# Shift taps of all channels as banded 128x128 products on TensorE, the filter loaded first, and a new instruction order

## The chip, the cores and the metric

The kernel runs on one core of a Trainium2 chip. TensorE (PE) multiplies, VectorE (DVE) and ScalarE (ACT) move results out of PSUM and do the elementwise work, GpSimd (POOL) does slower elementwise work, and SyncE (SP) issues the DMA transfers. The metric is the device time of one execution in microseconds. Times inside an execution are counted from the start of the profiled span.

## The reference, cut to what matters

Two kinds of layer alternate, A, B, A, B, over 2048 tokens of 512 channels. A is a gated long convolution: `k` is shifted by a 4-tap causal filter per channel, multiplied by `v`, convolved over the whole sequence with a filter as long as the sequence (plus a diagonal term), and gated by the normalized input. B is an MLP with 1376 hidden units.

```python
def _A_ref(q, k, v, shift_k, ssm_k, ssm_D):
    ...
    for t in range(ks):
        k_shift = k_shift + k_pad[:, t:t + S, :] * shift_k[:, ks - 1 - t][None, None, :]
    kv = k_shift * v
    ...                                    # y = kv convolved with ssm_k by FFT
    y = y + kv * ssm_D[None, None, :]
    return q * y

x = A_q
x = x + _A_ref(_layernorm(x, axis=-1), A_k, A_v, A_shift_k, A_ssm_k, A_ssm_D)
x = x + _B_ref(_layernorm(x, axis=-1), B_w1, B_b1, B_w2, B_b2)
...                                        # the same two once more
```

`k`, `v` and the filters do not depend on `x`, so both A layers share one convolution result Y, which is computed once, at the front.

## The kernel before, in words

**Layout.** A token is 16p + nt: partition p of 128 and row nt of 16. Channels run along the free dimension; they are handled in four tiles of 128, called cc 0 to 3 below, which before are 128 neighbouring channels each. All large buffers are views at fixed byte offsets into one tile, `arena`: `kn` (k), `uv` (v, then k shifted times v), `kT` (k transposed), `Kd` and `Zk` (the long filter), `ZX`, `ZK`, `KSW` (spectra), the MLP weights, and more.

**The front** (up to the first instruction of line L781) is a list of pieces, each with its engine, and with PSUM and SBUF slots; `_Plan.add` names a piece and its dependences, and `_Plan.write` emits the pieces in the order of the string `ORDER`. A word such as `KS60.P0` is piece KS60 on PE with PSUM slot 0; `.D`, `.A`, `.G` and `.S` mean DVE, ACT, POOL and SP. Each engine works strictly in its order of that list; a name with a trailing `e` is the eviction of the piece without it. There are four PSUM slots of 1024 float32 (`p`), nine small buffers `xb` and three large ones `ZT`. The pieces:

- `lk`, `lv`, `lF`, `lK..`, `lW`, `lM`, `lx`, `ly`, `w1` to `w4`: loads of k, v, the Fourier table, the long filter (four loads), the twiddle tables Wt and Mt, the input, the MLP weights. `lSK`, `lh..`: the taps, and k of the rows before.
- `wm0` to `wm2`: matmuls on the identity, without use of the result.
- The filter: `kd` adds the diagonal term to the first tap (32 elements per partition, 128 bytes apart), `KSab` is the first transform stage of 32 channels, 16 matmuls of half width each, `K2j` the second stage, `sa`, `sb` copies of the spectrum with the halves swapped (SBUF to SBUF).
- The taps, cc 0 to 2: `kT` transposes k on PE, `dg` makes diagonal 128x128 matrices of one tap each, `kv` adds up four products per block of tokens in PSUM, `kvm` multiplies the result by v (line L517). `bS` and `bSK` bring the taps into the right partitions. For cc 3: `kg`, `ka` and `kgm` do the multiplications and additions on POOL (L441, L443, L448, L452).
- The data transform of tile cc: `UccS` (four pieces with evictions into `ZT`, L302), `UccT` (turned by PE, or for cc 3 by DMA transposes), then four times `Xccj` (second stage, eviction into `xb`), `Tccj` (product with the filter's spectrum, L559), `Vccj` (inverse stage, L567), `Zccg` or `TD` (turned back), and `Y` (last inverse stage, L633).
- Around Y: `s00`, `s01`, `s02` normalize the first four rows of the input; `g` gates and adds, `h`, `p`, `b` normalize the result (statistics on DVE, power on POOL, application on DVE), `LT` transposes it and `M` is the first half of the first MLP group with its gelu. `LG1`, `q1`, `a1`, `g1.` to `b1.` do the same for the second group.

**The rest** (from L781 on) is written out in a loop over eight groups of 512 tokens, `mm1` (L747 with the gelu L749) and `mm2` (L781, its result added by DVE), four groups for each of the two MLP layers; the first `mm1` is what the pieces M did. The work between two groups (`prep`) belongs to DVE, POOL and SP.

Of the kernel before, what the change touches and what calls it, by code (L numbers as in the profile page):

```python
# [103 lines left out]
def kernel(ctx: ExitStack, tc: tile.TileContext, A_q, A_k, A_v, A_shift_k, A_ssm_k, A_ssm_D,  # L104
# [117 lines left out]
    class Stat:  # L222
# [27 lines left out]
        def apply(self, dst, g, a, b, src=None):  # L250
            for i in range(a, b):
                xs = x_t[:, GT * g + i, :] if src is None else src[:, i, :]
                nc.vector.tensor_scalar(out=dst[:, i, :], in0=xs, scalar1=self.mv[:, i, 0:1], scalar2=self.rs[:, i:i + 1],  # L253
                                        op0=ALU.subtract, op1=ALU.mult)
# [18 lines left out]
    with tc.tile_pool(name="ps", bufs=1, space=bass.MemoryType.PSUM) as ps:  # L273
# [73 lines left out]
        lS = [load("lSK", SKr, apf(A_shift_k, 0, [[D * KS, 1], [1, D * KS]]), 2 ** 13),  # L347
              load("lb1", b1r[:, 0:F], apf(B_b1, 0, [[F, 1], [1, F]]), 2 ** 13)]
        lS += [load(f"lh{p0}", kh[p0:p0 + n, :, :], apf(k_d, (16 * p0 - h) * D + CK * P, [[16 * D, n], [D, h], [1, P]]), 2 ** 17)
               for p0, n in ((1, 112), (113, 15))]  # L350

        def columns(o):
            for ct in range(CK):
                for t in range(KS):
                    nc.tensor.matmul(o[:, ct * KS + t:ct * KS + t + 1], at(81 * K + 2 * (ct * P * KS + t), [[KS, P]], 0, 1),
                                     one[0:1, 0:1], start=True, stop=True)
        _, sf = mm_evac("bS", 700, lS[:1], columns, [CK * KS], lambda: sF[:])

# [55 lines left out]
        for ct in range(CK):  # L414
            def diag(it, ct=ct):
                for t in range(KS):
                    dst, sc = DG[:, ct, t, :], sF[:, ct * KS + t:ct * KS + t + 1]
                    if it["eng"] == "A":
                        nc.scalar.activation(dst, IDt[:], AF.Copy, scale=sc)  # L419
                    else:  # L420
                        nc.vector.tensor_scalar(out=dst, in0=IDt[:], scalar1=sc, scalar2=None, op0=ALU.mult)
            dg.append(plan.add(f"dg{ct}", {"D": 600, "A": 1000}, [sf], diag))
        for q in range(4):
            def mms(o, q=q):
                for i in range(4):
                    for ct in range(CK):
                        nc.tensor.transpose(o[:, i, ct, :], kn[:, 4 * q + i, ct * P:ct * P + P], IDt[:])  # L427
# [5 lines left out]
        c3 = slice(CK * P, D)
        ksum, kpart = kn[:, :, 0:P], kn[:, :, P:2 * P]

        def sk(t, n):
            return apf(SK, t, [[P * KS, P], [0, n], [KS, P]])

        def tap(t):
            m = kpart if t else ksum  # L440
            nc.gpsimd.tensor_tensor(m[:, t:NT, :], kn[:, 0:NT - t, c3], sk(t, NT - t), ALU.mult)  # L441
            if t:
                nc.gpsimd.tensor_tensor(m[:, 0:t, :], kh[:, h - t:h, :], sk(t, t), ALU.mult)  # L443
        kg = []
        for t in range(KS):
            kg.append(plan.add(f"kg{t}", {"G": 4650 if t else 4100}, kg[-1:] if t else lk + lS[2:] + [bSK] + kTp, lambda it, t=t: tap(t)))
            if t:
                kg.append(plan.add(f"ka{t}", {"G": 4100}, kg[-1:], lambda it: nc.gpsimd.tensor_tensor(ksum, ksum, kpart, ALU.add)))  # L448

        def gmul(it):  # L450
            eng = nc.vector if it["eng"] == "D" else nc.gpsimd
            eng.tensor_tensor(uv[:, :, c3], uv[:, :, c3], ksum, ALU.mult)  # L452
# [406 lines left out]
```

## Time and profile before

| | |
|---|---|
| median of 3 runs | 246.73 us (246.53 to 247.12) |
| profiled execution | 246.67 us |
| its span | 244.8 us |
| granted TensorE clock | 1.0 |
| PE, DVE, ACT, POOL busy | 97%, 71%, 55%, 24% of the span |
| first instruction of L781 | 98.83 us |

Rows of the profile are read like this: line, engine, operation, output <- input, shapes, count, then busy time, mean duration of one in ns, and the idle time ahead with what ended it. Rows of the timeline begin with start and duration in us; in the chain, with the start and the time that the piece took in it. Rows of the windows give the stretch, its length, the busy time of PE, weight loads, DVE, ACT and POOL (with the number of instructions), the granted clock, the DMA engines' mean share and GB/s. A duration overlaps the next instruction's start, so the pace of a queue is read from starts.

### The profile page before, as it was taken

How to read it: one execution, taken by the hardware profiler on the slowest of the kernel's cores; microseconds unless marked ns; L12 is line 12 of the kernel's file. 1: busy time of each engine (PE TensorE's matmuls, PEld its weight loads, DVE VectorE, ACT ScalarE, POOL GpSimd, SP SyncE). 2: the span in 40 equal slices, each digit the busy share in tenths (PEclk: the TensorE clock that was granted, in tenths of full speed). 3: DMA queues.
4: the chain of work that ended last, by engine and by line, in shares of the span. 5: the costliest groups of instructions: out<-in, count | busy, mean ns of one | idle time of the engine just before them, and what ended most of it. 6: DMA issues, size and time to landing. Idle time of an engine off the chain costs nothing.

```text
span 244.8 us, 4913 instructions
## 1 busy us (share of the span) xinstructions
PE 236.3 (97%) x2002; PEld 142.0 (58%) x2002; DVE 172.6 (71%) x332; ACT 135.4 (55%) x194; POOL 59.4 (24%) x51
## 2 busy tenths in 40 slices
PE   6999999999997899999999999999999999999994
PEld 2799883789996587444444444444444444444443
DVE  0559699899997989979879898967856951021022
ACT  2538699899998999318307307406505604704700
POOL 2299999760000211310111111011001010000000
PEclk9999999999999999999999999999999999999999
DMA  7999994799998998050400404022024015011011
GB/s 232 329 217 221 170 426 168 265 364 216 260 182 159 269 153 251 3 86 1 85 0 3 87 0 86 3 47 40 0 68 107 0 44 127 3 43 43 0 43 43
DMA packets 56431, 29.64 MB, mean 121 GB/s; under 512 B 48883, under 2 KB 52696, under 8 KB 55514
## 3 DMA queue, kind: packets, MB, share of 16 engines
q1 hardware_dynamic: 56402, 29.34, 48.6%
q8 instruction: 15, 0.25, 0.4%
q14 instruction: 6, 0.05, 0.1%
q10 hardware_dynamic: 8, 0.00, 0.0%
HBM read 15.18 MB, written 2.10 MB: 71 GB/s over the span
## 4 chain that ended last, share of the span: by engine, by line
PE 79%; DVE 9%; ACT 8%; issue 2%; POOL 1%; DVEq 0%; ACTq 0%; POOLq 0%
PE po L781 31%; PE ph L747 27%; DVE arena L212 5%; PE p L509 4%; PE p L691 4%; ACT xb L210 3%; ACT arena L210 3%; PE p L408 2%; ACT ZT L210 2%; PE p L633 1%; PE p L427 1%; PE p L390 1%; PE p L302 1%; PE p L330 1%; DVE ZT L212 1%
## 5 line engine op out<-in xcount | busy, mean ns | idle before, releaser
L749 ACT ACTIVATE arena<-ph,B 128x512 bf16<-128x512 f32 (+1 forms) x77 | 52.8, 687 | 79.5 <-PE ph L747 79.4
L781 PE MATMUL po<-arena 128*128 128x512 bf16 (+2 forms) x363 | 77.4, 373 | 0.0
L747 PE MATMUL ph<-arena 128*128 128x512 bf16 (+1 forms) x308 | 67.6, 379 | 0.0
L781 PEld LDWEIGHTS <-arena 128*128 128x128 bf16 (+1 forms) x363 | 35.4, 98 | 40.6 <-POOL arena L818 0.3
L747 PEld LDWEIGHTS <-arena 128*128 128x128 bf16 (+1 forms) x308 | 30.8, 100 | 35.9
L786 DVE TENSOR_TENSOR arena<-po,arena 128x512 bf16<-128x512 f32 (+1 forms) x33 | 21.5, 671 | 42.6 <-PE po L781 42.5
L210 ACT ACTIVATE arena<-p 128x1024 bf16<-128x1024 f32 (+6 forms) x41 | 37.5, 993 | 8.2 <-PE p L427 5.4
L248 POOL TENSOR_TENSOR lrsm<-lrsm,mhalf 128x4 f32<-128x4 f32 (+2 forms) x11 | 10.1, 920 | 81.3 <-DVE lrsm L242 81.3
L210 ACT ACTIVATE ZT<-p 128x1024 bf16<-128x1024 f32 x21 | 21.5, 1133 | 6.4 <-PE p L302 6.2
L232 DVE BATCH_NORM_STATS2 lstm<-arena 128x6 f32<-128x512 bf16 x32 | 20.0, 681 | 0.3
L232 DVE BATCH_NORM_STATS2 lstg<-arena 128x6 f32<-128x512 bf16 x32 | 19.7, 676 | 0.0
L212 DVE CAST arena<-p 128x1024 bf16<-128x1024 f32 (+1 forms) x17 | 18.0, 1110 | 1.7 <-PE p L374 1.0
L248 POOL TENSOR_TENSOR lrsg<-lrsg,mhalf 128x4 f32<-128x4 f32 x8 | 8.1, 1011 | 43.1 <-DVE lrsg L245 43.0
L559 DVE TENSOR_TENSOR arena<-xb,arena 128x2048 bf16<-128x2048 bf16 (+1 forms) x16 | 17.6, 1151 | 0.9 <-ACT xb L210 0.9
L567 PE MATMUL p<-arena 128*128 128x128 bf16 x256 | 15.8, 219 | 0.5 <-ACT ZT L210 0.3
L441 POOL TENSOR_TENSOR arena<-arena,SK 128x2048 bf16<-128x2048 bf16 (+3 forms) x4 | 15.0, 3753 | 4.2 <-ACT DG L419 4.1
L253 DVE TENSOR_SCALAR arena<-arena,lmvg,lrsg 128x512 bf16<-128x512 bf16 x32 | 11.0, 408 | 6.8 <-POOL lrsg L248 6.8
L210 ACT ACTIVATE xb<-p 128x1024 bf16<-128x1024 f32 x15 | 15.2, 1119 | 0.7 <-PE p L544 0.7
L567 PEld LDWEIGHTS <-arena 128*128 128x128 bf16 x256 | 14.8, 98 | 1.1 <-DVE arena L559 0.5
L253 DVE TENSOR_SCALAR arena<-arena,lmvm,lrsm 128x512 bf16<-128x512 bf16 x32 | 11.5, 416 | 2.2 <-POOL lrsm L248 2.2
L448 POOL TENSOR_TENSOR arena<-arena 128x2048 bf16<-128x2048 bf16 x3 | 12.2, 4068 | 0.2
L509 PE MATMUL p<-DG,arena 128*128 128x128 bf16 x192 | 11.4, 219 | 0.0
(76 smaller groups left out, 224.8 us busy)
## 6 DMA issues: line engine op xcount, KB each, us to landing
arena<-arena SPq DMA_DIRECT2D x8, 512.0 KB, 5.9
arena<-in_A_k_dram SPq DMA_DIRECT2D x2, 1024.0 KB, 6.3
arena<-in_A_v_dram SPq DMA_DIRECT2D x2, 1024.0 KB, 9.6
arena<-in_A_ssm_k_dram SPq DMA_DIRECT2D x4, 512.0 KB, 9.1
arena<-tabM SPq DMA_DIRECT2D x1, 2048.0 KB, 10.3
out_dram<-arena SPq DMA_DIRECT2D x15, 128.0 KB, 1.7
arena<-in_A_q_dram SPq DMA_DIRECT2D x1, 1536.0 KB, 6.8
arena<-in_B_w_dram SPq DMA_DIRECT2D x1, 1376.0 KB, 7.8
```

Source lines behind the costliest of these rows:

```text
L210: nc.scalar.activation(dst, src, AF.Copy)
L212: nc.vector.tensor_copy(dst, src)
L232: nc.vector.bn_stats(self.st[:, i, 0, :], x_t[:, GT * g + i, :] if src is None else src[:, i, :])
L248: nc.gpsimd.tensor_tensor(self.rs[:, a:b], self.rs[:, a:b], mhalf[:, a:b], ALU.pow)
L253: nc.vector.tensor_scalar(out=dst[:, i, :], in0=xs, scalar1=self.mv[:, i, 0:1], scalar2=self.rs[:, i:i + 1], op0=ALU.subtract, op1=ALU.mult)
L509: nc.tensor.matmul(o[:, i, j, :], w, DG[:, cc, t, :], start=t == 0, stop=t == KS - 1)
L559: eng.tensor_tensor(kk, x2, kk, ALU.mult)
L567: nc.tensor.matmul(o[:, i, :], spec[:, cc, ka + i, :], Mt[:, ka + i, r, :], start=r == 0, stop=r == 1)
L747: nc.tensor.matmul(o.rearrange("p (i t) -> p i t", t=P), W1t[:, ct, ft * P:ft * P + m], lt[:, a:b, ct, :], start=ct == 0, stop=ct == CT - 1)
L749: nc.scalar.activation(hT[0:m, ft, a * P:b * P], o, AF.Gelu_apprx_tanh, bias=B1[0:m, ft:ft + 1])
L781: nc.tensor.matmul(po[:, a:b], hT[0:m, ft, i * P:(i + 1) * P], W2t[0:m, ft, a:b], start=ft == 0, stop=ft == FT - 1)
L786: nc.vector.tensor_tensor(xs, po[:, a:b], xs, ALU.add)
```

## The change

- **Tiles of channels.** Tile cc now holds every fourth channel, cc, cc + 4 and so on. Where U reads `uv` it takes `slice(cc, D, 4)`; the filter's KS evictions write `Zk` in that order; and Y, its evictions and the gates bring the channels back (`rows`, `rowd`).
- **Taps.** `kT` now transposes blocks of 4 rows by 32 channels, every 16th channel: 16 blocks for each of four groups of rows q. The contraction of a product then runs over (row, channel), and the four taps of 32 channels are one banded 128x128 matrix `DG`, whose part for the rows of the group before is 96 columns wide. `dg` builds it on POOL as a product of a small identity `ID4` with the taps `taps_t`, which four small loads `lT` bring with an offset of one tap for each 32 partitions. `DG` lies in the last four `xb` buffers, so all X pieces depend on all `kv`. Each `kv` piece is 16 matmuls; there are two for each of the four tiles, and two `kvm`. The pieces bS, bSK, lSK, lh, kg, ka and kgm are gone.
- **Four tiles for one buffer.** `arena` is cut at 96, 112, 128 KB into four tiles with the same layout.
- **Order.** `ORDER` is rewritten throughout. The filter's loads and its KS and K2 pieces come first; taps and data transform come after, tile 1 last instead of tile 3 in the U stage. On POOL stand dg (4), s01, T00 and T22 (before: T01); on ACT TD0a, TD0b, TD3 and Y32, Y30 before the gates' second half. `s02` moves to the end of the kvm pieces, `LG1` ahead of the first gate, Y32 and Y30 ahead of M0a. The SP order ahead of w1 is Z01 Z00 Z21 Z03 Z20 Z23 Z10 Z13 Z11 (before: Z00 Z01 Z20 Z21 Z10 Z11).

```diff
-    ROW = 149 * K // 2
-    arena = big.tile([P, ROW], BF16, name="arena")
+    PARTS = (0, 96, 112, 128, 149)
+    parts = [big.tile([P, (b - a) * K // 2], BF16, name=f"arena{a}") for a, b in zip(PARTS, PARTS[1:])]
...
+        lT = [load(f"lT{i}", taps_t[32 * i:32 * i + 32, :, i:i + KS],
+                   apf(A_shift_k, 0, [[NG4 * KS, 32], [KS, NG4], [1, KS]]), 2 ** 13) for i in range(4)]
...
+            _, e = mm_evac(f"KS{c // 2}{c % 2}", KSC, [kd, lF], mms, [8, P],
+                           lambda c=c: Zk.rearrange("p k (g m) -> p k g m", g=4)[:, :, :, 8 * c:8 * c + 8],
+                           src=lambda v: v.rearrange("p m (g k) -> p k g m", g=4))
...
+        DG = [view(xbb[NXB - CT + ct], [4, NU * 32]) for ct in range(CT)]
+        for ct in range(CT):
             def diag(it, ct=ct):
+                eng = nc.vector if it["eng"] == "D" else nc.gpsimd
+                eng.tensor_tensor(DG[ct].rearrange("p g (u c) -> p g u c", c=32),
+                                  apf(ID4, 0, [[32, P], [0, 4], [0, NU], [1, 32]]),
+                                  apf(taps_t, ct * NU, [[NG4 * NU, P], [CT * NU, 4], [1, NU], [0, 32]]), ALU.mult)
...
+                for g in range(NG4):
+                    nc.tensor.transpose(o[:, g, :], at(96 * K + 2 * (4 * q * D + g), [[NG4, P]]), IDt[:])
...
+        def taps(cc, o, deps):
+            def mms(v):
+                for e in range(4):
+                    for b in range(2):
+                        g, q = CT * e + cc, 2 * o + b
+                        before = kT[:, g, q - 1, 2:2 + P] if q else kT[:, g, 3, 1:1 + P]
+                        d = v[:, 2 * e + b, :]
+                        nc.tensor.matmul(d, kT[:, g, q, 2:2 + P], DG[cc][:, e, 0:P], start=True, stop=False)
+                        nc.tensor.matmul(d[:, 0:96], before, DG[cc][:, e, P:NU * 32], start=False, stop=True)
...
             def mul(it):
+                us = uv[:, 8 * o:8 * o + 8, :].rearrange("p i (c e x) -> p i c e x", e=4, x=4)[:, :, :, :, cc]
+                ks = view(pf[pe["slot"]["ps"]], [4, 8, 32]).rearrange("p e i c -> p i c e")
+                nc.vector.tensor_tensor(us, ks, us, ALU.mult)
...
+            sp, zu = first_stage(f"U{cc}", uv, slice(cc, D, CT), chunk(ZX, cc), [[um[cc][q // 2]] for q in range(4)], UT[cc] == "X", KWp)
```

The new order of each queue, as far as the prediction speaks of it:

```
SP:  lF lK11 lK00 lK01 lK10 lk0 lW lb1 lT3 lT1 lx0 lk1 lT0 lT2 lv0 lv1 lH sb2 sb1 sa2 sb3 sb0 sa0 sa1 lM sa3 U3T0 ly U3T1 lx
     Z01 Z00 Z21 Z03 Z20 Z23 Z10 Z13 Z11 w1 Z12 Z22 Z02 w3 w2 w4 LT3
PE:  wm0 kd6 KS70 KS60 kd0 KS61 KS00 KS11 KS10 KS01 kd2 KS71 KS21 KS20 KS30 kd4 KS31 KS51 KS40 KS41 KS50 kT0 kT1 K20 K211 ...
     kv00 K21 kv30 K213 kv01 U0S0 kv20 U3S0 U0S2 kv21 U0S1 kv11 U2S0 U0S3 kv31 U2S3 kv10 U2S2 U2S1 U0T0 ... X00 ...
     V33b V33a TD0a TD0b TD3 Y00 TD1 Y01 Y32 Y30 Y02 Y12 Y10 LT0 TD2 LT1 M0a M0b M1b M1a LT2 Y20 Y22 M2a M2c M2b
DVE: ... kvm00 kvm30 kvm01 kvm20 kvm21 kvm11 kvm31 kvm10 s02 U0T0e ... T33b T33a V32e LG1 g00 g01 h00 h01 b00 b01 g02 ...
ACT: ... V33be V33ae TD0ae TD0be TD3e Y00e Y01e TD1e Y32e Y30e Y02e Y12e LT0e TD2e LT1e Y10e M0ae ...
```

More of the change, by code (lines that the diff above doesn't have):

```diff
@@ new lines @@
+lF.S lK11.S wm0.P3 lK00.S kd6.P0 kd6e.D KS70.P1 KS60.P2 KS70e.A lK01.S kd0.P3 KS61.P0 kd0e.D KS00.P3 KS61e.A KS60e.D KS11.P1 KS10.P2 KS11e.A KS01.P0 lK10.S lk0.S kd2.P1 KS00e.D kd2e.A lW.S KS71.P3 KS10e.D lb1.S KS01e.A KS21.P1 lT3.S KS71e.D KS21e.A KS20.P2 KS30.P0 kd4.P3 kd4e.A lT1.S KS31.P1 KS30e.A KS20e.D KS51.P3 KS40.P2 KS31e.D KS40e.A KS41.P0 KS51e.D KS50.P1 kT0.P2 lx0.S lk1.S KS41e.A lT0.S kT1.P3 kT0e.A KS50e.D K20.P0 K211.P1 K22.P2 K20e.A K22e.A kT1e.D K28.P3 K212.P0 K211e.D K28e.D K23.P1 K212e.A K214.P2 K215.P3 K214e.D K23e.A bB.P0 K29.P1 lT2.S lv0.S lv1.S bBe.D K215e.A K25.P2 K29e.A K210.P0 kT3.P3 K25e.A s00.D K26.P1 K210e.A dg0.G kT2.P2 K26e.A K27.P0 kT3e.D K27e.A K24.P3 dg3.G kv00.P1 kT2e.D lH.S K21.P2 K24e.A sb2.S kv30.P0 dg2.G K21e.A K213.P3 kvm00.D kv01.P1 U0S0.P20 kvm30.D K213e.A kv20.P0 U3S0.P31 kvm01.D U0S0e.A dg1.G s01.G kvm20.D U3S0e.A U0S2.P1 kv21.P2 U0S1.P0 sb1.S sa2.S kv11.P3 U0S2e.A U0S1e.A U2S0.P12 kvm21.D U2S0e.A U0S3.P2 U0S3e.A kv31.P0 kvm11.D U2S3.P3 kvm31.D kv10.P1 U2S2.P2 U2S3e.A U2S2e.A U2S1.P0 kvm10.D sb3.S s02.D U2S1e.A U0T0.P3 U3S1.P1 sb0.S U3S2.P2 U0T0e.D sa0.S U2T0.P0 U2T0e.D U3S1e.A U3S3.P1 X00.P30 U3S2e.A U3S3e.A X00e.A U0T1.P2 X20.P01 sa1.S U1S0.P10 U2T1.P3 U0T1e.D X20e.A X02.P22 lM.S U2T1e.D U1S2.P0 U1S0e.A X03.P13 sa3.S U1S3.P3 X02e.A X03e.A U1S1.P2 X21.P14 U1S2e.D U1S1e.A U1S3e.D U3T0.S X21e.A X22.P05 X23.P26 X01.P37 T00.G X22e.A T03.D X01e.A T02.D V00.P1 X23e.A U1T0.P0 ly.S V03.P3 V00e.A U3T1.S T20.D V02.P2 V03e.A T01.D U1T1.P1 U1T0e.D X30.P38 V01.P0 V02e.A U1T1e.D X11.P20 X30e.A X10.P13 T22.G V01e.A X12.P32 X11e.D T23.D V20.P02 X10e.A T21.D X13.P21 V22.P1 X12e.A X13e.A V22e.A V23.P3 T10.D V20e.A V21.P2 lx.S V23e.D X31.P17 Z01.S V21e.A Z00.S V10.P00 X33.P35 X32.P26 Z21.S T11.D X31e.A T12.D Z03.S V10e.A Z20.S X32e.A wm2.P1 V11.P1 V12.P0 T13.D T30.D V11e.A V13.P2 V12e.A V30.P11 T31.D V13e.A wm1.P0 X33e.A V30e.A T32.D Z23.S Z10.S T33b.D V31.P2 Z13.S V32.P0 T33a.D Z11.S V33b.P3 V33a.P1 w1.S V32e.D V31e.A V33be.A V33ae.A TD0a.P2 TD0b.P3 TD3.P0 TD0ae.A TD0be.A Y00.P1 LG1.D Z12.S TD3e.A Y00e.A TD1.P2 Y01.P3 g00.D q1.G Y32.P0 Y01e.A g01.D Z22.S h00.D TD1e.A Z02.S h01.D p00.G b00.D p01.G Y32e.A Y30.P1 Y02.P2 Y30e.A b01.D Y12.P3 Y10.P0 LT0.P1 Y02e.A g02.D Y12e.A TD2.P2 h02.D LT1.P3 LT0e.A p02.G w3.S a1.D w2.S TD2e.A LT1e.A M0a.P1 M0b.P2 M1b.P3 Y10e.A M0ae.A b02.D g10.D M1be.A M1a.P0 M0be.A LT2.P1 h10.D Y20.P3 LT2e.A Y22.P2 w4.S M2a.P1 g12.D Y20e.A M1ae.A M2c.P3 Y22e.A M2ce.A p10.G h12.D p12.G M2ae.A M2b.P0 b12.D b10.D M2be.A LT3.S
@@ L132 @@
     rot = ctx.enter_context(tc.tile_pool(name="rot", bufs=2))
-    ROW = 149 * K // 2
-    arena = big.tile([P, ROW], BF16, name="arena")
+    PARTS = (0, 96, 112, 128, 149)
+    parts = [big.tile([P, (b - a) * K // 2], BF16, name=f"arena{a}") for a, b in zip(PARTS, PARTS[1:])]
+    arena, ROW = parts[0], (PARTS[1] - PARTS[0]) * K // 2
     def at(off, dims, p0=0, n=P):
-        return apf(arena, p0 * ROW + off // 2, [[ROW, n]] + dims)
+        i = max(i for i in range(len(parts)) if off >= PARTS[i] * K)
+        row = (PARTS[i + 1] - PARTS[i]) * K // 2
+        return apf(parts[i], p0 * row + off // 2 - PARTS[i] * K // 2, [[row, n]] + dims)
     def place(name, shape, off):
@@ L182 @@
     nc.gpsimd.memset(b1r[:, F:FT * P], 0.0)
-    h = KS - 1
-    nc.gpsimd.memset(kh[0:1, :, :], 0.0)
+    for i in range(4):
+        nc.gpsimd.tensor_copy(ID4[32 * i:32 * i + 32, :], IDt[32 * i:32 * i + 32, 32 * i:32 * i + 32])
     nc.gpsimd.memset(mhalf[:], -0.5)
@@ L346 @@
         lF = load("lF", Ft[:], F_h.ap().bitcast(BF16), 2 ** 17)
[L347 to L357, printed above, removed]
+        lb = load("lb1", b1r[:, 0:F], apf(B_b1, 0, [[F, 1], [1, F]]), 2 ** 13)
+        lT = [load(f"lT{i}", taps_t[32 * i:32 * i + 32, :, i:i + KS],
+                   apf(A_shift_k, 0, [[NG4 * KS, 32], [KS, NG4], [1, KS]]), 2 ** 13) for i in range(4)]
         def bias(o):
@@ L398 @@
                        for w, a in (("a", 0), ("b", 1))])
-        _, bSK = mm_evac("bSK", 250, lS[:1], lambda o: nc.tensor.matmul(o, one[:], SKr[:, CK * P * KS:], start=True, stop=True), [P * KS],
-                         lambda: SK[:])
         IDw = apf(IDt, 0, [[P, P], [0, 4], [1, P]])
@@ L413 @@
         kTp, kTe, dg = [], [], []
-        for ct in range(CK):
+        DG = [view(xbb[NXB - CT + ct], [4, NU * 32]) for ct in range(CT)]
+        for ct in range(CT):
             def diag(it, ct=ct):
[L416 to L422, printed above, removed]
+                eng = nc.vector if it["eng"] == "D" else nc.gpsimd
+                eng.tensor_tensor(DG[ct].rearrange("p g (u c) -> p g u c", c=32),
+                                  apf(ID4, 0, [[32, P], [0, 4], [0, NU], [1, 32]]),
+                                  apf(taps_t, ct * NU, [[NG4 * NU, P], [CT * NU, 4], [1, NU], [0, 32]]), ALU.mult)
+            dg.append(plan.add(f"dg{ct}", {"D": 1000, "G": 2000}, lT, diag))
@@ L430 @@
+            pe, ev = mm_evac(f"kT{q}", 1250, [lk[q // 2]], mms, [NG4, P], lambda q=q: kT[:, :, q, 2:2 + P], True)
             kTp.append(pe)
             kTe.append(ev)
[L433 to L452, printed above, removed]
@@ L512, in taps @@
             kvp.append(pe)
-            lo, hi = nts[0], nts[-1] + 1
             def mul(it):
-                us = uv[:, lo:hi, ccs[0] * P:(ccs[0] + n) * P].rearrange("p i (j c) -> p i j c", c=P)
-                nc.vector.tensor_tensor(us, view(pf[pe["slot"]["ps"]], [len(nts), n, P]), us, ALU.mult)
-            return plan.add("kvm" + name, {"D": 1150}, [pe, lv[lo // 8]], mul, free=[(pe, "ps")])
-        um01 = [taps(f"0{q}", (0, 1), range(4 * q, 4 * q + 4), [kTe[q], kTe[q - 1]]) for q in range(4)]
@@ L520 @@
-        um2 = [taps(f"2{o}", (2,), range(8 * o, 8 * o + 8), [kTe[2 * o], kTe[2 * o + 1], kTe[2 * o - 1]]) for o in range(2)]
+                us = uv[:, 8 * o:8 * o + 8, :].rearrange("p i (c e x) -> p i c e x", e=4, x=4)[:, :, :, :, cc]
+                ks = view(pf[pe["slot"]["ps"]], [4, 8, 32]).rearrange("p e i c -> p i c e")
+                nc.vector.tensor_tensor(us, ks, us, ALU.mult)
+            return plan.add(f"kvm{cc}{o}", {"D": 1150}, [pe, lv[o]], mul, free=[(pe, "ps")])
+        um = [[taps(cc, o, [kTe[2 * o], kTe[2 * o + 1], kTe[2 * o - 1]]) for o in range(2)] for cc in range(CT)]
```

70 lines of the change are left out of this document (27 added, 43 removed).

## The prediction

> **What bounds the kernel now.** I read the page's busy table and chain first, then the chain in order of time, then the windows, then the queues of ScalarE (ACT), VectorE (DVE) and SyncE (SP).
>
> ```profile
> PE 236.3 (97%) x2002; PEld 142.0 (58%) x2002; DVE 172.6 (71%) x332; ACT 135.4 (55%) x194; POOL 59.4 (24%) x51
> PE 79%; DVE 9%; ACT 8%; issue 2%; POOL 1%; DVEq 0%; ACTq 0%; POOLq 0%
> ```
> ```profile
> 2.08 5.44 PE p L408 x13
> ...
> 11.68 5.36 PE p L509 x96
> ...
> 83.57 0.41 PE p L641 x4
> ...
> 84.65 1.95 PE p L691 x32
> 86.60 0.22 PE p L641 x4
> ...
> 90.57 1.73 PE p L633 x8
> ...
> 98.83 9.52 PE po L781 x44
> ...
> 231.91 9.56 PE po L781 x55
> ```
>
> From 98.83 on TensorE does the dense matmuls back to back to the end: a fixed block that the change does not touch. All that can move is the front, 0 to 98.83 us, so I predict when L781 starts. In the front the page's "PE 97%" misleads, since idle shorter than a matmul's tail is counted busy. The windows tell more (the four columns after PEld are DVE, ACT, POOL, clock):
>
> ```profile
> 12.00:18.00 6.00, 5.99 (x113) 5.68 (x112) 3.23 (x5) 1.77 (x3) 6.00 (x2) 1.00 0.96 207
> 18.00:24.00 6.00, 6.00 (x109) 5.54 (x104) 6.00 (x12) 4.97 (x6) 5.92 (x3) 1.00 0.95 235
> 24.00:30.00 6.00, 5.95 (x125) 5.34 (x124) 4.18 (x4) 3.92 (x6) 5.84 (x4) 1.00 1.12 178
> 66.00:72.00 6.00, 6.00 (x109) 5.99 (x107) 6.00 (x7) 6.00 (x8) 0.00 (x0) 1.00 1.07 149
> ```
> ```profile
> 17.59 1.02 ACT L210 ACTIVATE ZT<-p 128x1024 bf16<-128x1024 f32 x1 [4.23 <-PE p L302]
> 54.59 4.70 ACT L210 ACTIVATE xb<-p 128x1024 bf16<-128x1024 f32 x5
> 59.10 1.10 ACT L210 ACTIVATE arena<-p 128x1024 bf16<-128x1024 f32 x1
> 37.56 7.02 DVE L212 CAST arena<-p 128x1024 bf16<-128x1024 f32 x6
> 57.99 9.16 DVE L559 TENSOR_TENSOR arena<-xb,arena 128x2048 bf16<-128x2048 bf16 x8
> 76.31 1.36 DVE L212 CAST ZT<-p 128x512 bf16<-128x512 f32 x2
> 78.40 1.37 DVE L253 TENSOR_SCALAR arena<-arena,lmvg,lrsg 128x512 bf16<-128x512 bf16 x4
> 79.80 0.69 DVE L660 TENSOR_TENSOR arena<-arena,p 128x512 bf16<-128x512 bf16 x1
> ```
>
> Up to 30 us TensorE is the bound (96 of the 192 tap matmuls stand there in a row) and the two eviction engines starve: in 12 to 30 us DVE is idle for 4.6 us and ACT for 7.3. Later both are full: the front is then a queue of PSUM evictions. Their real price is start to start: ACT does five in 59.10 - 54.59, so 0.902 each (0.907 over longer runs); DVE (7.02 - 1.22) / 5 = 1.16, and 1.13 for a product L559. The last V evictions end at 77.67 (call it T), then s02 (78.40) holds DVE until the first gate g00 at 79.80, M0a starts at 84.65 and L781 at 98.83.
>
> **The change, part by part.** Rows for the prices (page, groups with shapes kept apart, timeline, windows of 1 us, transfers):
>
> ```profile
> L441 POOL TENSOR_TENSOR arena<-arena,SK 128x2048 bf16<-128x2048 bf16 (+3 forms) x4 | 15.0, 3753 | 4.2 <-ACT DG L419 4.1
> L448 POOL TENSOR_TENSOR arena<-arena 128x2048 bf16<-128x2048 bf16 x3 | 12.2, 4068 | 0.2
> L517 DVE TENSOR_TENSOR arena<-p,arena 128x1024 bf16<-128x1024 f32 x6 | 7.3, 1222 | 3.6 <-PE p L509 3.6
> L212 DVE CAST ZT<-p 128x1024 bf16<-128x1024 f32 x6 | 7.3, 1216 | 0.1
> L212 DVE CAST arena<-p 128x32 bf16<-128x32 f32 x2 | 0.6, 304 | 1.0 <-PE p L374 1.0
> L373 PE MATMUL p<-arena,IDt 128*128 128x32 bf16 x4 | 0.9, 216 | 0.1
> L374 PE MATMUL p<-Dz,IDt 128*128 128x32 bf16 x4 | 0.8, 196 | 0.0
> ```
> ```profile
> 8.82 1.45 ACT L210 ACTIVATE arena<-p 128x1536 bf16<-128x1536 bf16 x1 [5.39 <-PE p L427]
> 10.16 1.51 PE L427 MATMUL p<-IDt,arena 128*128 128x128 bf16 x24
> 33.27 2.19 PE L380 MATMUL p<-Ft,arena 128*64 128x128 bf16 x64
> 20.75 2.46 DVE L232 BATCH_NORM_STATS2 lstg<-arena 128x6 f32<-128x512 bf16 x4
> 15.57 10.21 SPq L341 DMA_DIRECT2D arena<-in_A_ssm_k_dram  x3
> 70.31 6.28 SPq L613 DMA_TRANSPOSE arena<-ZT  x4
> 76.70 0.52 SPq L278 DMA_DIRECT2D arena<-in_B_w_dram  x1
> arena<-in_B_w_dram SPq DMA_DIRECT2D x1, 1376.0 KB, 7.8
> ```
> ```profile
> 25.00:26.00 1.00, 1.00 (x28) 0.91 (x23) 1.00 (x1) 0.44 (x2) 1.00 (x1) 1.00 1.35 214
> 29.00:30.00 1.00, 0.95 (x30) 0.82 (x26) 0.72 (x1) 1.00 (x2) 1.00 (x1) 1.00 0.24 37
> 31.00:32.00 1.00, 0.97 (x31) 0.84 (x27) 1.00 (x2) 0.94 (x3) 1.00 (x1) 1.00 0.95 401
> ```
>
> *GpSimd's taps go* (27.2 us of POOL in L441 and L448). POOL is 1% of the chain, so by itself that is worth nothing; it lets the last channel tile start early. POOL gets four dg products of 896 elements, at 4068 ns for 2048 about 1.8 us each, and two T products where it had one, which takes 1.13 us off DVE.
>
> *The taps on TensorE.* 192 matmuls become 128 (96 of 128 columns, or all of them, at the 57 ns of 5.36 / 96): 7.3 us for 10.8. Transposes rise from 48 to 64 at 61 ns (1.51 less its 0.05 tail, over 24). The columns and bSK matmuls with their evictions and the 12 diagonal scalings go too; the sum below is made from the new queues, in which they no longer stand. Transposed k grows to 4 evictions of 2048: one on ACT, 1.9 by 1.45 x 2048/1536, three on DVE at 1.13 to 1.2. The product with v becomes 8 instructions for 6.
>
> *Two operands that become strided.* (a) kvm reads and writes uv at one element in 8 bytes. Lower bound: no cost, as ZT's cast, which writes pieces of 8 bytes, 1216 ns against L517's 1222. Upper bound: kd's eviction of 32 elements at 128-byte steps takes 304 ns, where 0.17 + 32 x 1.03 ns is 0.20: 3.2 ns an element, or 3.3 us for each kvm. I take 0: its spacing is nearest to ZT's. (b) The kT transposes load weights at 32-byte steps. L373, whose moving operand steps 128 bytes, takes 20 ns more than the dense L374, 0.63 ns an element, so up to 80 ns for 128, or 1.3 us for each kT; lower bound 0. I take 40 ns, the spacing being between the two.
> [...]
>
> *Filter first.* ACT's first eviction stays at about 8.8 us: wm0 runs to 7.6, kd6 and one KS follow. A filter load is 524 KB at 214 GB/s, 2.45 us; the 10.21 us that three of them hold SP show pauses between (the 29 to 30 row, 37 GB/s), so four take 11 to 13 us from about 1.8. Then lk0 and lW, 2.1 MB at 401: lW is there at 20 to 21.5. The KS stage costs TensorE 0.53 per tile of 16 and the two evictors 16 x 0.51 together, so it ends at 18.5 to 19; then kT0, kT1, and K2's first eviction starts at 20.5. The taps' loads, lk1 and lv, come later but under K2's evictions.
>
> *The queues in the new order.* ACT up to the last V: 63 evictions of 1024 (8 KS, 13 K2, 14 U, 15 X, 13 V) x 0.907 = 57.1, kT0 1.9, two kd 0.5, two half V 1.0: 60.5. DVE: 24 at 1.16, nine 2-byte ones at 1.13, T 13 x 1.13 + 1.2, s00 2.8, s02 1.4, kd and bB 0.8: 58.9. I laid the pieces down in queue order: each begins when its engine is free, its input written and its PSUM slot emptied. Checkpoints: KS done 18.6, K213 evicted 32.6, first kvm 30.0 to 31.2, last kvm 41.3, X00 evicted 46.0, V00 55.1, T 73.5. ACT idles 4.2 us after 8.8: 1.8 in KS, 0.3 at kT0, 1.7 waiting for kvm, 0.4 at the end. Check: 8.8 + 60.5 + 4.2 = 73.5. To this I add 1.3 (lW and the strided transposes delay K2) and 0.8 for handovers, which my laying down ignores (issue is 2% of the chain, of 66 us). T = 75.6, against 77.67.
>
> *The tail.* s02 leaves it (done at about 43), but V33b, V33a, TD0a, TD0b and TD3 now all stand on ACT ahead of Y00e, which g00 waits for: PE 0.35 + 0.3 + 0.8 + 1.0 + 0.6 = 3.1, for 2.1 before. g00 at 78.7 (79.80). Both gates and statistics now precede b00, and ACT has Y01e, TD1e and four Y evictions before LT0e (0.5 + 5 x 0.9): M0a 5.8 after g00 (4.85 before), at 84.5. Y30, Y32 and LT1 move ahead of M0a into PE's wait, so M0a to L781 shrinks from 14.18 by 1.73 + 0.22 to 12.2: L781 at 96.7. LG1 (2.95) fits while DVE waits.
> w1 is next to be late: nine transposes of 1.57 (four in 6.28) stand ahead of it instead of six; from V21's eviction on they run to 76.5, and 7.8 later is 84.3, no slack beside 84.5. lM is issued only after the last tap, at about 40: 2.1 MB at 401 is 5 us, in time for V00's matmuls at 52 unless the swaps ahead of it hold it 6 us. X now waits for all taps too, since DG lies in its buffers: the last tap ends at 40, X00 starts at 44. The split of the arena and Zk's order cost nothing: same sizes, runs of 16 bytes instead of 64.
>
> *Sum.* 98.83 - 96.7 = 2.1 off. The profiled run took 246.67 (span 244.8 plus 1.9 around it), the median of the three is 246.73: 246.67 - 2.1 = 244.5.
>
> **The rivals.** *Strided kvm, slower.* In the U stage ACT waits for kvm, so after about 1 us of slack every extra tenth on a kvm is 0.8 us. It undoes the gain at (2.1 + 1) / 8 = 0.39 us each, 0.38 ns an element; at a quarter of kd's price, 0.8 ns, it is 6.6 - 1 on top: 250.1; at all of it about 270. For: kd's row. Against: ZT's, and that POOL's L441 reads SK at 8-byte steps in 2.02 ns an element (3753 for a mean of 1856) and the dense L448 in 1.99.
> *Filter first starves.* If the four filter loads take 3.4 us each by SP's 10.21, and lk0 and lW see a pause too, K2 starts at 24 to 24.5, ACT idles 3 us more than I allowed, and T is 78 to 79: 247.3 to 249.
> *Hidden anyway.* The front shrinks but w1 lands 2 us later: the end stays at 246.3 to 247.1. For: the transposes' queue; against: fewer of them run beside w1 (three left, six before).
> *Better.* Loads in time, transposes at no extra: T 73.5 to 74.3, and w1 early with it: 242.6 to 243.3.
>
> **How the numbers follow.** My case (243.3 to 246.1) 0.47; better 0.18; hidden 0.12; starving 0.11; strided kvm 0.12. 0.2% (0.5 us) is about what this kernel's measurement can tell from no change. Faster 0.65, same 0.12, slower 0.23. The range leaves out kvm's case and the ends of the better and starving ones: 241.8 to 248.2; the likeliest case's own is 243.3 to 246.1.
>
> **What will show it.** L517's successor near 1.22 us each (right) or above 1.6 (wrong); transposes of kT at 61 to 140 ns start to start; K2's first matmul at 20 to 22; ACT busy 90% from 9 to 75; the first gate at about 78.7, the first gelu matmul at 84.5 and who released it (LT0e or w1); the first L781 at 96.7, and the same 142.6 us from there to the last matmul. Wrong if DVE becomes the engine that all wait for at 30 to 45, or if a DMA ends the wait ahead of K2 or M0a for over 2 us.

## The result, and the profile after

The change made the kernel slower: 256.73 us median (255.45 to 257.38, 6 runs) against 246.44 us before (246.15 to 247.12, 6 runs), a ratio of 1.0411, 95% interval 1.0383 to 1.0439. The prediction was 244.5 us, 241.8 to 248.2. The profiled execution after took 255.45 us, its span 253.6. It is the fastest of the six, 8.8 us above before's profiled execution, so the trace shows all but 1.5 us of the 10.3 between the medians.

First the page of after: the busy line, the clock that TensorE was granted in 40 slices, the chain's shares by engine, and two groups of VectorE (busy us, mean ns of one).

```profile
PE 234.0 (92%) x1941; PEld 140.1 (55%) x1941; DVE 178.3 (70%) x316; ACT 140.1 (55%) x197; POOL 37.6 (15%) x49
...
PEclk9999997999999999999999999999999999999999
...
PE 66%; DMA 12%; DVE 10%; SPq 5%; ACT 4%; issue 2%; DVEq 0%; ACTq 0%
...
L522 DVE TENSOR_TENSOR arena<-xb,arena 128x2048 bf16<-128x2048 bf16 (+1 forms) x15 | 20.1, 1404 | 0.0
...
L483 DVE TENSOR_TENSOR arena<-p,arena 128x1024 bf16<-128x1024 f32 x8 | 18.6, 2502 | 0.4 <-PE p L475 0.4
```

L483 is the product with v (kvm), L517 before: 2502 ns a piece, where it was 1222 in the same shape. L522 is T, L559 before: the mean rose from 1151 to 1404 ns. Two rows of before for comparison, T on its page and kvm's only piece in its chain:

```profile
L559 DVE TENSOR_TENSOR arena<-xb,arena 128x2048 bf16<-128x2048 bf16 (+1 forms) x16 | 17.6, 1151 | 0.9 <-ACT xb L210 0.9
...
27.36 0.91 DVE arena L517
```

Now the chain of after, in order of time; L752 is L781 before.

```profile
13.98 8.57 DMA Wt<-tabW
...
34.99 6.88 DVE arena L483 x3
...
44.19 2.52 DVE arena L483
...
48.53 10.80 DMA arena<-arena
...
89.96 0.70 DVE arena L631
...
94.56 0.40 PE p L610 x4
...
95.81 4.91 PE p L662 x88
...
107.70 9.51 PE po L752 x44
```

The gelu group's second matmul starts at 107.70, 8.87 us later than the 98.83 of before, and the dense block behind it is as long as it was. So the front alone is longer. In it the first gate (89.96) is 10.2 us late, and VectorE's kvm hold 11.1 us of the chain (the two rows of L483 and one of 1.67 between them), where in before's chain they held 0.91. The timeline of VectorE and ScalarE shows the two places where it goes wrong (start, duration, idle time ahead and what ended it).

```profile
32.73 18.58 DVE L483 TENSOR_TENSOR arena<-p,arena 128x1024 bf16<-128x1024 f32 x8 [0.41 <-PE p L475]
...
60.42 8.49 DVE L522 TENSOR_TENSOR arena<-xb,arena 128x2048 bf16<-128x2048 bf16 x4
...
40.12 1.94 ACT L211 ACTIVATE ZT<-p 128x1024 bf16<-128x1024 f32 x2 [2.43 <-PE p L303]
...
71.19 1.02 ACT L211 ACTIVATE arena<-p 128x1024 bf16<-128x1024 f32 x1 [3.41 <-DVE arena L213]
```

The eight kvm run back to back from 32.73 to 51.3 (32.73 + 18.58), and ScalarE starves behind them. Then four T take 8.49 us, where the same four at 1.2 would take 4.6. The next view is all instructions of line L522: minimum, median and maximum in ns.

```profile
L522 DVE TENSOR_TENSOR arena<-xb,arena x15: 685/1218/5091, 60.4 to 84.8; 128x2048 bf16<-128x2048 bf16 x13, 128x1024 bf16<-128x1024 bf16 x2
...
L522 POOL TENSOR_TENSOR arena<-xb,arena x2: 4073/4207/4341, 55.9 to 62.4; 128x2048 bf16<-128x2048 bf16 x2
```

One T on VectorE took 5091 ns. The timeline shows it beside T22 on GpSimd:

```profile
62.36 4.34 POOL L522 TENSOR_TENSOR arena<-xb,arena 128x2048 bf16<-128x2048 bf16 x1 [2.44 <-ACT xb L211]
...
62.69 5.09 DVE L522 TENSOR_TENSOR arena<-xb,arena 128x2048 bf16<-128x2048 bf16 x1
```

T22 ends at 66.70 (62.36 + 4.34), and VectorE's T at 67.78 (62.69 + 5.09), 1.08 us later, which is about what one T takes.

### The profile page after: what moved, and what is told of

It reads as the page before. It is cut to its first block, busy times and chain, and to the rows that moved or that the text cites. A ratio compares the mean times of both kernels' runs of the same rounds, so it can differ in the third digit from the quotient of the medians.

```text
span 253.6 us, 4775 instructions
## 1 busy us (share of the span) xinstructions
PE 234.0 (92%) x1941; PEld 140.1 (55%) x1941; DVE 178.3 (70%) x316; ACT 140.1 (55%) x197; POOL 37.6 (15%) x49
## 4 chain that ended last, share of the span: by engine, by line
PE 66%; DMA 12%; DVE 10%; SPq 5%; ACT 4%; issue 2%; DVEq 0%; ACTq 0%
PE po L752 30%; PE ph L718 26%; DMA arena<-in_A_v_dram 4%; DVE arena L483 4%; DMA arena<-arena 4%; PE p L662 4%; SPq L342 4%; DMA Wt<-tabW 3%; DVE arena L522 3%; PE p L530 2%; ACT ZT L211 2%; SPq L279 2%; PE p L507 1%; ACT xb L211 1%; ACT arena L211 1%
## 5 line engine op out<-in xcount | busy, mean ns | idle before, releaser
L752 PE MATMUL po<-arena 128*128 128x512 bf16 (+2 forms) x363 | 77.4, 372 | 0.0
L752 PEld LDWEIGHTS <-arena 128*128 128x128 bf16 (+1 forms) x363 | 35.4, 98 | 40.5
L211 ACT ACTIVATE arena<-p 128x1024 bf16<-128x1024 f32 (+7 forms) x45 | 39.8, 983 | 13.6 <-PE p L373 5.7
L211 ACT ACTIVATE ZT<-p 128x1024 bf16<-128x1024 f32 (+1 forms) x25 | 24.1, 1026 | 7.5 <-PE p L303 7.4
L213 DVE CAST arena<-p 128x1024 bf16<-128x1024 f32 (+1 forms) x13 | 13.2, 1077 | 11.1 <-PE p L367 9.0
L522 DVE TENSOR_TENSOR arena<-xb,arena 128x2048 bf16<-128x2048 bf16 (+1 forms) x15 | 20.1, 1404 | 0.0
L530 PE MATMUL p<-arena,arena 128*128 128x128 bf16 x256 | 16.2, 219 | 3.7 <-DVE arena L213 3.5
L483 DVE TENSOR_TENSOR arena<-p,arena 128x1024 bf16<-128x1024 f32 x8 | 18.6, 2502 | 0.4 <-PE p L475 0.4
L303 PE MATMUL p<-Ft,arena 128*128 128x256 bf16 x64 | 10.0, 291 | 3.1 <-DVE arena L483 3.0
L213 DVE COPY arena<-p 128x2048 bf16<-128x2048 bf16 x9 | 10.7, 1218 | 2.8 <-PE p L416 1.7
```

Of the source, the lines that this page charges most:

```text
L211: nc.scalar.activation(dst, src, AF.Copy)
L213: nc.vector.tensor_copy(dst, src)
L483: nc.vector.tensor_tensor(us, ks, us, ALU.mult)
L522: eng.tensor_tensor(kk, x2, kk, ALU.mult)
L530: nc.tensor.matmul(o[:, i, :], spec[:, cc, ka + i, :], Mt[:, ka + i, r, :], start=r == 0, stop=r == 1)
L752: nc.tensor.matmul(po[:, a:b], hT[0:m, ft, i * P:(i + 1) * P], W2t[0:m, ft, a:b], start=ft == 0, stop=ft == FT - 1)
```

## The experiments

Two theories. A: the product with v is dear because it is strided (2.51 for 1.22 us), and that is the greater part of the loss. B: the loss comes from loads and their order (Wt late, lM and the shift sa3 late) and from the T products on GpSimd, and kvm is hidden.

**The product on neighbouring channels (e1).**

```diff
-                nc.vector.tensor_tensor(us, ks, us, ALU.mult)
+                ud = uv[:, 8 * o:8 * o + 8, cc * P:cc * P + P].rearrange("p i (c e) -> p i c e", e=4)
+                nc.vector.tensor_tensor(ud, ks, ud, ALU.mult)
...
-            sp, zu = first_stage(f"U{cc}", uv, slice(cc, D, CT), ...
+            sp, zu = first_stage(f"U{cc}", uv, slice(cc * P, cc * P + P), ...
```

> The eight products with v (kvm, L483) work in place on 128 neighbouring channels of uv instead of every fourth one, and the U stage then takes its weights from those columns; nothing else changes. v is thereby multiplied with the taps of other channels, so only the time is of interest. Theory A (the element step of 8 bytes makes kvm dear, 2.51 us for 1.22, and that is most of the loss): kvm falls to 1.2 to 1.3 us, the last of them ends at about 42 instead of 51.3, TensorE no longer waits at 35 to 48 and its granted clock stays at 1.00 there; 8 x 1.14 = 9.1 us come back less what other waits take in its place (K2's late start and the waits at the T stage stay): 246 to 249. Rival B (the loss comes from loads, the late lM and sa3, and the T products on GpSimd): kvm gets faster but the first gelu matmul stays later than 104, and the time falls by less than 3 us, to 253 or more.

Measured: 249.78 us, ratio to before 1.0126 (1.0091 to 1.0162). kvm:

```profile
L484 DVE TENSOR_TENSOR arena<-p,arena 128x1024 bf16<-128x1024 f32 x8 | 9.7, 1224 | 1.4 <-PE p L475 1.4
```

7.0 us of the 10.3 lost come back. Theory A holds for the greater part; the time is 0.8 us above its range, and of what is left T22's block (e3) is the greater part: one T still takes 5.1 us here. The prediction did not weigh a third change in kvm: its PSUM operand is no longer read in order (in `ks`, elements read one after another lie 1 KB apart). e1 keeps that and takes 1224 ns, where before took 1222 with PSUM read in order, so this costs nothing.

**Read strided, write dense (e2).**

```diff
+    uw = place("uw", [P, CT, NT, P], 96 * K)
...
+                ud = uw[:, cc, 8 * o:8 * o + 8, :].rearrange("p i (c e) -> p i c e", e=4)
-                nc.vector.tensor_tensor(us, ks, us, ALU.mult)
+                nc.vector.tensor_tensor(ud, ks, us, ALU.mult)
...
-            sp, zu = first_stage(f"U{cc}", uv, slice(cc, D, CT), ...
+            sp, zu = first_stage(f"U{cc}", uw[:, cc], slice(0, P), ...
```

> kvm still reads every fourth channel of uv, but writes its product densely into a buffer of its own, and the U stage reads its weights from there. One of the two strided operands is left. If each strided operand adds the same (1.29 us over 1.22, so 0.64 each), kvm is about 1.86 us and the time lies about half way, 249.5 to 252. If the write alone is what costs, kvm is 1.2 to 1.3 and the time is that of the dense kernel, 246 to 249. If the read alone costs, kvm stays at 2.4 to 2.5 and so does the time, 255 to 257. Rival B: under 2 us whatever kvm takes.

Measured: 250.72 us, 1.0151 (1.0125 to 1.0176).

```profile
L485 DVE TENSOR_TENSOR arena<-p,arena x8: 1224/1224/1225, 32.9 to 42.4; 128x1024 bf16<-128x1024 f32 x8
```

All eight take 1224 or 1225 ns, as in e1, with the read still at every fourth channel. The read costs nothing by itself, so it takes the written step to make kvm dear (that step with a dense read was not tried). The time is 1.7 us above the range given for this case and would fit a kvm of 1.86 us as well; it is kvm's own duration that decides. The time lies within e1's spread (248.0 to 251.1).

**T00 and T22 back on VectorE (e3).** In ORDER:

```diff
-T00.G ... T22.G
+T00.D ... T22.D
```

> After's kernel with the two T products that it gives to GpSimd (T00, T22) back on VectorE. In the trace of after one T on VectorE takes 5.09 us while T22 runs on GpSimd, where others take 1.22: 3.9 us lost, against 2 x 1.13 us that VectorE now has to do itself. Theory A: all T take 1.2 us, the front ends 0 to 3 us earlier: 253.5 to 256.5. Rival B (the block is a main cost and what replaces it lies in idle time): 3 to 4 us, 252.5 to 253.5. If the long one was not due to GpSimd, one T stays at about 5 us and the time rises by 1 to 2 us.

Measured: 253.05 us, 1.0269 (1.0244 to 1.0295), 3.7 us less than after.

```profile
L522 DVE TENSOR_TENSOR arena<-xb,arena x17: 680/1214/1219, 62.0 to 84.2; 128x2048 bf16<-128x2048 bf16 x15, 128x1024 bf16<-128x1024 bf16 x2
```

The longest of 17 is 1219 ns: the 5.09 us was GpSimd's doing. The gain is at B's end of the expectation, so the block lay almost wholly on the path: in this part B was right.

**The shift sa3 ahead of lM (e4).** In ORDER: lM and sa3 change places.

> After's kernel with one change of order on SyncE's queue: the shift sa3 is issued ahead of the 2.1 MB load lM, not behind it. In the trace of after lM leaves at 48.2, sa3 at 48.5, and the first T on VectorE starts only at 60.4, at the end of a 10.8 us transfer in the chain. Theory A: this is a consequence of the late kvm and worth little, since evictions on ScalarE go on meanwhile: 0 to 1 us, 254.5 to 257. Rival B: T starts at 55 to 57 and the front gains 2 to 4 us: 252.5 to 254.5.

Measured: 257.17 us, 1.0421 (1.0392 to 1.0449): no change. The first T on VectorE starts at 60.82, for 60.42 in after. After's chain had named the transfer (the row at 48.53, which is sa3's), but VectorE was busy with PSUM evictions up to that moment anyway: of two things that end at the same time a chain names one.

**Both steps, not in place (e5).** kvm reads uv and writes a second buffer of the same layout, both at every fourth channel.

> kvm reads every fourth channel of uv, as in after, and writes every fourth channel of a second buffer of the same layout, from which the U stage takes its weights at the same 8-byte step as in after. Both steps stay; only the product is no longer in place. Theory A (the write at 8-byte steps of 2 bytes is dear, whatever it writes over): kvm 2.4 to 2.5 us, time as after, 255.5 to 257.5. Rival (what is dear is the in-place strided product, each element read and written back in the same place): kvm 1.2 to 1.3 us, time as the kernel that writes densely, 249.5 to 251.5.

Measured: 257.7 us, 1.0444 (1.0413 to 1.0475).

```profile
L485 DVE TENSOR_TENSOR arena<-p,arena 128x1024 bf16<-128x1024 f32 x8 | 18.6, 2494 | 0.4 <-PE p L476 0.4
```

As dear as in place, so it is the spacing of the written elements and not the reuse of their place.

**Wt ahead of k (e6).** In ORDER: `lW` ahead of `lk0`, and K20, K211, K22, K28 ahead of kT0 and kT1, with their evictions.

> After's kernel with the load of Wt issued ahead of the first half of k, and the first four K2 products ahead of kT0 and kT1 in the queues of TensorE, ScalarE and VectorE. In the trace of after K2's first matmul at 22.6 waits for Wt. Theory A (the late start of K2 is a loss of its own): K2 starts at 20 to 20.8, everything behind it moves by 1.5 to 2 us, 254.5 to 255.5. Rival (the taps and v, which stand behind these loads, bind kvm anyway): the first kvm stays at 32.5 to 33, time within 0.5 us of after, 256 to 257.2.

Measured: 257.35 us, 1.0438 (1.0408 to 1.0468): nothing, as the rival had it. K2 starts at 19.64 instead of 22.60, but then kT0 waits for k, and the first kvm begins at 33.13 (32.73 in after).

```profile
19.64 1.89 PE L383 MATMUL p<-arena,Wt 128*128 128x512 bf16 x7 [1.72 <-DVE arena L213]
22.46 2.21 PE L416 MATMUL p<-IDt,arena 128*128 128x128 bf16 x32 [0.93 <-DMA arena<-in_A_k_dram]
```

**Dense write and both T on VectorE (e7).** The edits of e2 and e3 together.

> The dense write of kvm and both T products on VectorE together. If the two losses stand one behind the other, 250.7 - 3.7 gives 247.0, within 1 us. If they share cover (with VectorE freer after the kvm it waits elsewhere), 248 to 250. Under 246 would mean that each alone was masked by the other.

Measured: 246.0 us, 0.9974 (0.9958 to 0.9989) of the 246.37 of before in that comparison. The two losses stand one behind the other, and with both gone the changed kernel is level with before or a little better. Together the edits give 10.7 us, apart 6.0 (e2) and 3.7 (e3). Of B only T22 is left: the loads stand in after's order here, and the loss is gone.

**T00 left on GpSimd (e8, e9).** e9 has the dense write and of e3 only T22; e8 has Wt first as in e6 as well.

> Dense write of kvm, Wt first with four K2 ahead of kT, T22 on VectorE, but T00 left on GpSimd, where in the traces of after and of the dense-writing kernel it ran beside VectorE's PSUM evictions and no VectorE instruction was long. If GpSimd's product blocks only VectorE's products of two SBUF operands, T00 saves 1.1 us of VectorE at no price, and with 1.5 to 2 us of Wt's order: 243.5 to 245.5, faster than before (246.6). If the load order is worth nothing: 245.5 to 247. If T00 costs as T22 did, one T at 5 us and 248 or more.

> Dense write of kvm, T22 on VectorE, T00 left on GpSimd, loads in after's order. Against the kernel with both products on VectorE (246.0) it tells what T00 on GpSimd is worth: if it saves its 1.13 us of VectorE on the path, 244.8 to 245.3; if nothing, 245.7 to 246.3. Against the same kernel with Wt loaded ahead of k (245.4) it tells what that order is worth: with after's trace K2 started 3 us earlier but kT stood in the middle of it, so I expect 0 to 0.4 us, 245.3 to 245.8.

Measured: e8 245.39 us, 0.9958 (0.9941 to 0.9975); e9 245.41 us, 0.9944 (0.9926 to 0.9962). T00 on GpSimd blocks nobody: the four T that took 8.49 us in after take 4.63 in e9.

```profile
53.11 4.63 DVE L524 TENSOR_TENSOR arena<-xb,arena 128x2048 bf16<-128x2048 bf16 x4
```

e8 against e7, on the same chip, puts T00's worth at 0.6 us, with intervals that overlap, and only if Wt's order, which e8 has as well, is worth nothing. e8 against e9 shows no worth of that order, though these two ran on different chips.

**Seven K2, and six K2 with one between the transposes (e10, e12).** Queue orders only: in e10 seven K2 stand ahead of kT1 and kT0; in e12 six, then kT0, K23 (evicted by VectorE), kT1.

> As e8 (Wt ahead of k), but seven K2 products instead of four stand ahead of kT0 and kT1, so that both eviction engines have work until k lands at about 22.5. In the trace of e8 ScalarE and VectorE idle 1.4 and 1.6 us there. If K2's late start is a loss of its own, the front gains 1 to 1.5 us on e8: 243.9 to 244.5. If the taps or kvm bind next, nothing: 245 to 245.8.

> As e10, but six K2 products ahead of kT0 and one between kT0 and kT1, whose eviction goes to VectorE, so that the 2.2 us in which TensorE does the 32 transposes find both eviction engines with work. In e9 and e10 ScalarE idles 2.5 and 2.7 us at 20 to 26 and the time is the same. If that idle time is what keeps the front from the predicted length, it falls to under 1.5 us and the time to 244 to 245. If DVE or the taps bind next, 245.2 to 245.8 as e9 and e10.

Measured: e10 245.39 us, 0.9942 (0.9922 to 0.9962); e12 244.39 us, 0.9904 (0.9877 to 0.9931), the fastest that ran. e10 is a miss: ScalarE's pauses only moved. In e12 they were not under 1.5 us either. ScalarE's timeline of e12:

```profile
20.20 2.85 ACT L212 ACTIVATE arena<-p 128x1024 bf16<-128x1024 f32 x3 [1.47 <-PE p L384]
23.71 5.78 ACT L212 ACTIVATE arena<-p 128x2048 bf16<-128x2048 bf16 x5 [0.66 <-PE p L417]
30.24 1.02 ACT L212 ACTIVATE arena<-p 128x1024 bf16<-128x1024 f32 x1 [0.75 <-PE p L384]
31.66 3.89 ACT L212 ACTIVATE arena<-p 128x1024 bf16<-128x1024 f32 x4 [0.40 <-PE p L384]
35.76 1.02 ACT L212 ACTIVATE ZT<-p 128x1024 bf16<-128x1024 f32 x1 [0.20 <-PE p L304]
```

The pauses add up to 3.5 us (2.7 in e9 from 18.6 to U's first eviction), and U's first eviction at 35.76 is no earlier than e9's 35.28. What took the place of Wt's wait is in the chain of e12:

```profile
18.25 10.25 DMA arena<-in_A_k_dram
...
28.55 1.22 PE p L417 x16
```

The second half of k lands at 28.5, and kT3 follows it. Work drawn forward does not shorten the front while k, and the taps behind it, come no earlier. The 1.0 us between the medians of e12 and e9 has no counterpart in these two profiles (first L754 at 97.43 and 97.03) and their intervals overlap. The profiled run of e12 (245.15 us) is one of the slowest of its six and that of e9 (244.96) one of the fastest of its ten, so the two profiles can't tell. That e12 beats before is measured, that its order beats e9's is open.

**Half the step (e11).** As e9, with two tiles interleaved in the second buffer, so that kvm writes every second element, 4 bytes apart.

> As e9, but the products with v are written at every second element, 4 bytes apart, two channel tiles interleaved in the second buffer (the U stage takes its weights at that step). Theory A (a write that is not contiguous costs a full extra hop per element): kvm 2.4 to 2.5 us as at 8 bytes, time near that of after with T22 on VectorE, 252 to 254. Rival (the cost grows with the step): kvm 1.5 to 1.9 us, 247.5 to 250. If 4 bytes are free as the read at 8 bytes is: 1.22 us and 245.4.

Measured: 244.94 us, 0.9927 (0.9900 to 0.9954).

```profile
L485 DVE TENSOR_TENSOR arena<-p,arena x8: 1312/1324/1334, 32.6 to 42.1; 128x1024 bf16<-128x1024 f32 x8
```

0.10 us more than dense. Both of the first two expectations are missed, the last is nearly met: the price jumps between 4 and 8 bytes (1324 ns here, 2502 in after), and no step between the two was run.

## Why the prediction was wrong

**The failed step is "(a) kvm reads and writes uv at one element in 8 bytes ... I take 0".** The right value was 2502 - 1222 = 1.28 us each. The rival "Strided kvm, slower" had the mechanism and the point from which it decides, 0.39 us each; at 1.28 its own working gives 244.5 + 8 x 1.28 - 1 = 253.7, and e3, in which kvm is the only one of the two losses left, measured 253.05. What misled was the choice of nearest row. ZT's cast writes 8-byte pieces, which is four elements side by side, and SK's rows are read by GpSimd; kvm writes single elements. The lower bound was drawn from the byte distance, with a row whose four elements side by side cost nothing extra (1216 ns); single elements written 8 bytes apart took 2502, and 4 bytes apart 1324 (e11), so run length and distance both count. The upper bound, kd's 3.2 ns an element, came from a write of single elements (304 ns, for 0.20 us by an estimate from before's casts to ZT, 692 ns for 512 elements and 1216 for 1024), and the measured 1.28 / 1024 = 1.25 ns lies within the bounds; but the range left that case out with a chance of 0.12.

**The second failed step is "two T products where it had one, which takes 1.13 us off DVE".** T00 did that. T22 began while VectorE was at its own T, and one of these lasted 5.09 us: 3.7 us lost in after (e3, which moves both products), and where kvm is mended 4.7 against e7 (250.72 - 246.0, both moved) and 5.3 against e9 (250.72 - 245.41, T22 alone). These runs are on different chips, on which before's medians differ by up to 0.5 us. Before's T01 on GpSimd stood beside PSUM evictions, so no row of before showed the block, and the prediction gave it no bound. It alone would have put the sum at the upper end of the range.

**Filter first: late, but not the loss.** Wt landed at 22.55 (13.98 + 8.57), not at 20 to 21.5, and K2's first matmul came at 22.60, not at 20 to 22. e6, e8 and e10 drew it forward by 2.4 to 3.0 us for no gain, so the time that the prediction gave to "Filter first starves" (3 us of ScalarE lost) was not lost: kT0, kT1 and k stood next.

**Strided weights (b)** were taken at 40 ns each. The weight loads did rise, 98 ns before (first row) to 148 in after:

```profile
L427 PEld LDWEIGHTS <-arena 128*128 128x128 bf16 x48 | 2.7, 98 | 0.3 <-issue 0.2
...
L416 PEld LDWEIGHTS <-arena 128*128 128x128 bf16 x64 | 4.3, 148 | 1.7 <-DMA arena<-in_A_k_dram 1.5
```

But 32 transposes took 2.21 us (e6's row above), and less the tail of 0.15 that a single one has beyond its pace they go at 64 ns. The 61 of the prediction had a tail of only 0.05 in it, which no run shows; worked out with the tail of 0.15 (one lasts 219 ns), before's 24 in 1.51 us go at 57. So the step costs about 8 ns each, 0.5 us for all 64, where 40 ns each is 2.6. The term was too high and lay mostly beside other work.

**lM** was in time: the first V matmul follows the first T, at 61.42 in after and at 53.90 in e9 (52 predicted), and what it waits for there is VectorE (lM, issued at 48.16 in after, lands 8.3 us later). The order of lM and sa3 is worth nothing in after (e4); without the late kvm it was not tried.

**The tail was right.** From the last V evictions (87.0 in after: 84.13 + 2.88) to L752 it is 107.70 - 87.0 = 20.7 us, for 96.7 - 75.6 = 21.1 predicted; M0a to L752 is 11.9 for 12.2; M0a followed LT0 and not w1. So *Hidden anyway* is out too.

**The sum without the two steps.** e9 differs from the change by the dense write and T22 alone. Its first L754 is at 97.03 and its profiled run took 244.96 us, for 96.7 and 244.5 predicted; its median is 245.41, a gain of 0.56% (0.38 to 0.74) where 0.9% was forecast. The closeness of 97.03 is in part luck: the last V evictions end at 76.3 for 75.6 predicted, and the tail of 20.7 us, 0.4 shorter than predicted, makes up for half of that.

## What to carry to other kernels

Where an operand's layout changes, ask for reads and writes apart how many neighbouring elements each touches and how far apart, and bound the cost by a row that has both alike on the same side of the same engine, not by one with the same byte distance alone. Before handing an elementwise product to GpSimd, look at what VectorE does in that stretch: in after it was free beside VectorE's PSUM evictions (1.22 to 1.23 us each beside T00) and dear beside a VectorE product of two SBUF operands (5.09 us for 1.22 beside T22). When the chain names a transfer, check whether the waiting engine was busy up to that moment before taking the transfer for the cause.

## What the runs showed of the hardware that was not expected

**Writes and reads at a step are not alike.** kvm, 1024 elements of 2 bytes, its other source in PSUM: dense 1224 ns (e1); read at 8 bytes and written dense 1224 (e2); read at 8 and written at 4 bytes 1324 (e11); read and written at 8 bytes 2489 to 2502 (after and e3 to e6). So the read at 8 bytes cost nothing, and beside that read the write cost 0.10 us at 4 bytes and 1.27 to 1.28 at 8. Why the write costs what it does, no run shows.

**A product on GpSimd held up one on VectorE.** VectorE's T lasted 5091 ns beside T22 in after, and 1226 at most in the runs without T22 on GpSimd; T00 (4.07 us) lengthened nothing, with PSUM evictions of 1.22 to 1.23 us beside it. That the blocked T waits for T22's end is an inference from times: it ends 1.08 us after T22 does, and T on VectorE go at 1.13 us start to start. The wait stands inside the blocked instruction's duration (5091 ns) and not as idle time (0.0 us ahead of L522).

**The granted clock fell in some profiles where TensorE had waited, and not in others.** After's windows (the columns are those of before's) around the first kvm:

```profile
37.00:38.00 1.00, 0.45 (x5) 0.45 (x6) 1.00 (x2) 0.69 (x1) 0.49 (x3) 0.79 1.03 389
38.00:39.00 1.00, 1.00 (x14) 1.00 (x12) 1.00 (x1) 0.00 (x0) 0.00 (x0) 0.50 1.01 373
...
41.00:42.00 1.00, 0.81 (x16) 0.72 (x14) 1.00 (x2) 1.00 (x2) 0.00 (x0) 1.00 1.02 381
```

e5's kvm is as slow and TensorE waits in the same stretch, but its clock stays at 1.00, and its span is 254.2 us for after's 253.6. So these two profiles show no cost of after's fall, though e5's three other runs, at a mean clock of 0.985 to 0.993 for its 0.998, took 1.7 to 1.9 us longer. In e3 the page's slice from 18.9 to 25.3 shows a clock of 7 tenths, with a wait of 1.85 us for Wt in it, and in e4 and e6 the slice from 70.2 to 76.6 shows 7 tenths, behind T22's block. And e2, where T22's block comes earlier and TensorE idles behind it:

```profile
57.00:62.00 5.00, 2.56 (x46) 2.38 (x43) 5.00 (x2) 3.73 (x5) 2.98 (x1) 1.00 1.14 239
62.00:66.00 4.00, 2.61 (x25) 2.71 (x26) 2.46 (x3) 0.71 (x1) 0.00 (x0) 0.52 0.91 228
66.00:70.00 4.00, 4.00 (x48) 4.00 (x47) 3.76 (x4) 2.43 (x4) 0.00 (x0) 0.62 1.07 102
```

In e2 the clock is at 0.52 to 0.62 from 62 to 70, just where TensorE is needed again; in e7, without the block, it is 1.00 there. e1's profile has the same block (four T in 8.49 us, for 8.51 in e2, behind which TensorE idles 3.5 us, for 3.8 in e2) and no such fall, and its span is 247.4 us for e2's 249.4. So the length of the wait alone doesn't decide. All six runs of e2 had a mean clock of 0.985 to 0.993, all twelve of e7 0.998 to 1.000. In e2 the block costs 4.7 us and in after 3.7: the clock may be the difference, which no run took apart.
